# Batch 0 of a packed-attention kernel: its second softmax with tokens on the partitions, in two parts, and a new written order of the opening steps

## The chip, the core and the metric

The kernel runs on one core of a Trainium2 chip. The metric is the device time of one execution in microseconds (us). Shown times are medians of several runs. One more execution was recorded by the hardware profiler; its rows give the time inside the kernel, from the first instruction of the program (0 us).

The engines are named as in the profile: PE is TensorE (matmuls; PEld are its weight loads), DVE is VectorE, ACT is ScalarE, POOL is GpSimd, and SP is the engine whose queue issues the DMAs (SPq). Each takes its instructions in the order in which they were written.

## The reference

Eight batches, eight heads, 576 tokens, head dimension 64, and 32 packed queries `p` for each head:

```python
def sm_attn(qq, kk, vv):
    s = scale * np.matmul(qq, kk.transpose(0, 1, 3, 2))
    a = np.exp(s - np.max(s, axis=-1, keepdims=True))
    a = a / (np.sum(a, axis=-1, keepdims=True) + 1e-09)
    return np.matmul(a, vv)
p_packed = sm_attn(p, k, v)               # 32 x 64 for each head
out = sm_attn(q, p_packed, p_packed)      # 576 x 64 for each head
x = out.transpose(0, 2, 1, 3).reshape(8 * 576, 512)
result = (x @ w_a * (x @ w_b)) @ w_out    # w_a, w_b: 512 x 1536; w_out: 1536 x 512
```

All is fp32. The kernel multiplies in a faster matmul format (fp32r) and restores precision by splitting an operand into a high and a low part, so a product costs three matmuls: high by high, high by low, low by high.

## The kernel before, in words

**The algebra.** The second attention's output is never formed. Let `a2` be its softmax weights (256 rows, that is 8 heads by 32 packed queries, and 576 token columns, kept as two tiles `e` = 0, 1 of 128 rows). `p_packed` is multiplied into `w_a` and `w_b` once for each batch (G, `g_tiles`, high and low parts `ghi` and `glo`), and `a2` is multiplied by G (`mm1`). The 1536 hidden columns are cut into 12 tiles `ft` of 128. For each, `mm1` makes two products (one for w_a, one for w_b), ScalarE copies the first out of PSUM, VectorE multiplies it by the second, ScalarE rounds the high part `h_hi`, GpSimd makes the low part `h_lo`. `mm2` multiplies h by `w_out`.

**Batch 0** is written by its own list. Batches 0 and 1 use this plain form; later batches use another one and are not touched by the change.

**The steps.** `FIRST` is the order of the first loads on SP's queue: `p0`, `k0`, `k1`, `q0`, `q1` (four heads each, 512 KB), `k2`, `q2` (the last 64 tokens of all heads), `v0`, `v1`, and `w1` for one piece of the weights. `START` is the order in which the opening steps are written for all engines. In it:

- `k0`..`k4`, `q0`..`q4`: `turn_first`, TensorE turns a loaded piece and `TURN` says whether VectorE (0) or ScalarE (1) copies it out of PSUM. `T0`: p turned (`pT`). `P0`: p_packed turned (`ppT`).
- `S0`, `S1`, then `r0`, `r1` (four each): first softmax (`stage1`), for `e` = 0 and 1: scores; maximum and exponent; reciprocal of the sum; turns of the weights and two copies of them (`a1T`) on ScalarE; product with v, scaled into `pp`.
- `s0`, `s1` (seven each): the steps of the second softmax (`stage2`), one call for each `e`. Scores with the 32 packed queries of four heads on the partitions; a stream transpose by VectorE, so that the 32 values of a softmax lie side by side, and the maximum; subtraction; exponent on ScalarE; sum, reciprocal and the multiplication by it; a stream transpose back (`a2f`) and the high part of `a2` on ScalarE; the low part on VectorE (`lo_part`, L91). `SUBS` says whether subtraction and multiplication go to VectorE (1) or GpSimd (0).
- `A`, `B`, `C`: a weight piece comes as 64-bit numbers. `A` (high word) runs on ScalarE, `B` (low word) on the engine that `WAYS` gives for this piece (0 ScalarE, 1 VectorE, 2 GpSimd), `C` (`both_words`, L205) on VectorE. Each `C` frees a buffer and lets SP issue the next piece; twelve pieces fit. `D` splits a `w_out` piece.
- `W`: `warm`, dummy matmuls. `g`: G of the first two `ft` tiles, which needs the first four `C`. `Lk2`, `Lv2`, `Lp2` and the like: loads of batch 1.

After `START` the loop over `ft` begins. `mm1` calls `between()` twice for each `ft`; each call writes the steps that `PLAN_0` holds for that slot (weight pieces, batch 1's attention). At odd `ft`, `g_tiles` makes G for the next two tiles. For `ft` = 0, `mm1` first does the half of both products that needs `e` = 0 alone.

PSUM is held in three sets: `x` (two single banks), `m` (two pairs of banks), `s` (one pair). The order on every engine is the written one (a manual schedule); semaphores are added where data or a buffer must be waited for.

Of the kernel before, what the change touches and what calls it, by code (L numbers as in the profile page):

```python
# [12 lines left out]
ALU = mybir.AluOpType  # L13
# [6 lines left out]
def tile_packed_attn_gated_ffn(  # L20
# [69 lines left out]
    def lo_part(dst, src, hi, eng=nc.vector):  # L90
        return eng.tensor_tensor(out=dst, in0=src, in1=hi.bitcast(F32), op=ALU.subtract)  # L91
# [93 lines left out]
    def xT_cols(b, key, u, h, cols=slice(0, HS)):  # L185
        return xTs[b, key][h // R][64 * u:64 * u + 64, h % R, cols]
# [60 lines left out]
    def stage1(b, e):  # L247
# [59 lines left out]
            nc.vector.tensor_scalar(out=pp[b][:, i, :], in0=pps[:, 0:D], scalar1=rs, scalar2=None, op0=ALU.mult)  # L307
        yield

    def stage2(b, e):  # L310

        TU = 2 * XH
        x = bank_pair(b > 0 or e == 0)
        for r in range(R):
            for u in range(2):
                nc.tensor.matmul(  # L316
                    out=x[J * r:J * r + J, u, 0:HS], lhsT=ppT[64 * u:64 * u + 64, 1 if u ^ e else 2 * (b % 2), r, :],
                    rhs=xT_cols(b, "q", u, 2 * r + e), start=True, stop=True)
        yield
        s2 = work(b, f"s2_{e}", [P, TU, J], "t1")  # L320
# [6 lines left out]
        eng = nc.vector if b < 2 and SUBS[2 * b + e] == "1" else nc.gpsimd  # L327
        eng.tensor_tensor(out=s2, in0=s2, in1=mx.unsqueeze(2).broadcast_to([P, TU, J]), op=ALU.subtract)
# [5 lines left out]
        nc.vector.tensor_reduce(out=total, in_=s2, axis=AX, op=ALU.add)  # L334
        nc.vector.tensor_scalar(out=sum2, in0=total, scalar1=1e-9, scalar2=None, op0=ALU.add)
        nc.vector.reciprocal(out=sum2, in_=sum2)
        eng.tensor_tensor(out=s2, in0=s2, in1=sum2.unsqueeze(2).broadcast_to([P, TU, J]), op=ALU.mult)
# [12 lines left out]
        yield  # L350
# [27 lines left out]
                lo_part(lo, part, hi)  # L378


    def mm1_half(i, ft, ps=None, kts=range(E)):

        ps = bank_pair() if ps is None else ps
        cols = slice(P * i, P * i + P)
        steps = [(gt, at, kt) for kt in kts for gt, at in ((ghi, a2_hi), (ghi, a2_lo))]
        steps += [(glo, a2_hi, kt) for kt in kts]
        for n, (gt, at, kt) in enumerate(steps):
            for half in range(2):
                nc.tensor.matmul(  # L389
                    out=ps[:, half, 0:HS], lhsT=gt[:, kt, ft % 4, cols], rhs=at[:, kt, HS * half:HS * half + HS],  # L390
                    start=(n == 0 and kt == 0), stop=(n == len(steps) - 1 and kt == E - 1))
        return ps

    def mm1(b, ft, between):
        asb = sm.tile([P, 2, HS], F32, name="asb")
        if b == 0 and ft == 0:
            pa, pb = (mm1_half(i, ft, kts=(0,)) for i in range(2))
            mm1_half(0, ft, pa, (1,))
        else:
            pa, pb = mm1_half(0, ft), None  # L400
# [101 lines left out]
    WAYS = ("000000022220202120012012011200010010")  # L502
    TURN = ("0001110101")
    SUBS = ("0100")

    PLAN = (" |  |  | S0 | r0 | r0 |  | r0 |  | r0 Lv1 ; S1 | r1 | r1 q0 Lk2 | r1 | r1 | q1 Lk3 Lv2 P0 |  ; s0 | s0 s0 | s0 T2 | "
            "s0 Lp4 | s0 s1 | s1 s1 | s1 | s1 | s1 | t0 t1 t2 t3 u0 | k2 |  | k3 Lq2")
    PLAN = dict(enumerate(PLAN.split("|")))
    PLAN_0 = ("A | C C | B A B A | B C C B C | A A | C | B | C B A T0 k0 Lp2 A | A A B B C Lq0 | C C k1 | A B A | "
# [3 lines left out]
    PLAN_0 = dict(enumerate(PLAN_0.split("|")))  # L513

    pieces = [(c, n) for c in range(NC) for n in range(4)] + [(NC, f) for f in range(NFT)]
# [38 lines left out]
            del raws[c, n]  # L554
            load_pieces(2)

    def warm(n=9):

        x = bank_pair()[:, 0, :]
        t = firsts["k", 0].rearrange("p h t -> p (h t)")  # L560
        for _ in range(n):
            nc.tensor.matmul(out=x, lhsT=ident, rhs=t[:, 0:512], start=True, stop=True)
# [74 lines left out]
    for b in range(NB):  # L637
# [318 lines left out]
```

## Time and profile before

| | before |
|---|---|
| median of 3 runs | 714.15 us (713.82 to 714.51) |
| the profiled execution | 714.0 us |
| its span, first to last instruction | 712.2 us |
| PE, PEld busy | 699.0 us (98%), 574.2 us (81%) |
| DVE, ACT, POOL busy | 449.8 us (63%), 363.2 us (51%), 417.8 us (59%) |
| moved by DMA | 102.37 MB |

In the rows of the timeline the first number is the start in us, the second the time from the start of the first to the end of the last instruction that the row holds, then come engine, source line, operation, what is written from what, the shape and the count (x8 is eight instructions), and in brackets the idle time before it with what ended it. Busy times overlap on PE, since matmuls are pipelined. An fp32 matmul is two instructions, a turn by TensorE one. A row of the busy times by stretch has the stretch, its length, the busy time and count for PE, PEld, DVE, ACT and POOL, the granted clock, the share of the DMA engines and GB/s. A row of the chain of waits has start, duration, engine, tile and line. A row of the groups by line has the form, the count, the busy time and the mean duration in ns.

### The profile page before, as it was taken

Reading aid. Unit: us, or ns where it says so; the run is one execution under the profiler, and the core shown is the slowest. Engines: PE = TensorE matmul, PEld = TensorE weight load, DVE = VectorE, ACT = ScalarE, POOL = GpSimd, SP = SyncE. Lnnn points to the kernel's source line nnn. Section 1 sums busy time; section 2 is a strip of 40 time slices with the busy share of each in tenths; the row PEclk is TensorE's granted clock in tenths of the full one; section 3 lists DMA queues with packets and bytes.
Section 4 is the critical chain, followed back from the end, with each engine's and each line's share of the span. In section 5 each row is a group of like instructions: output and inputs, shape, how many; then the busy total and the mean of one; then the engine's idle time right before and its main releaser. Section 6 shows DMA issues by size and latency. Waiting matters only on the chain.

```text
span 712.2 us, 14198 instructions
## 1 busy us (share of the span) xinstructions
PE 699.0 (98%) x5558; PEld 574.2 (81%) x5558; DVE 449.8 (63%) x819; ACT 363.2 (51%) x733; POOL 417.8 (59%) x322
## 2 busy tenths in 40 slices
PE   6899999999999999999999999999999999999998
PEld 4488877888778887887888788788888888888887
DVE  3888755367455669665875668765785657754342
ACT  3788753554344455644563456554554455544520
POOL 0496753337334687745874579566776578856520
PEclk9999999999999999999999999999999999999999
DMA  8999872767344735555453574457146323133002
GB/s 230 387 274 315 220 162 53 193 153 282 93 98 139 211 96 141 139 138 146 134 111 115 142 195 93 106 176 182 61 98 180 105 89 119 61 110 127 1 1 74
DMA packets 177059, 102.37 MB, mean 144 GB/s; under 512 B 141280, under 2 KB 159456, under 8 KB 171616
## 3 DMA queue, kind: packets, MB, share of 16 engines
q1 hardware_dynamic: 176992, 101.47, 50.3%
q8 instruction: 43, 0.70, 0.4%
q14 instruction: 24, 0.20, 0.1%
HBM read 85.72 MB, written 15.73 MB: 142 GB/s over the span
## 4 chain that ended last, share of the span: by engine, by line
PE 94%; DVE 2%; SPq 1%; DMA 1%; ACT 1%; issue 0%; DVEq 0%; ACTq 0%
PE x L724 37%; PE m L765 29%; PE m L389 9%; PE x L779 5%; PE m L415 5%; PE s L301 2%; PE s L316 1%; PE s L255 1%; PE x L371 1%; PE s L291 1%; SPq L116 1%; DMA kn<-in_k_dram 1%; DMA nat<-in_k_dram 0%; PE m L152 0%; PE x L152 0%
## 5 line engine op out<-in xcount | busy, mean ns | idle before, releaser
L724 PE MATMUL x<-wo,h_hi 128*128 128x512 f32 (+1 forms) x776 | 249.3, 391 | 0.0
L91 POOL TENSOR_TENSOR h_lo<-asb,h_hi 128x576 fp32r<-128x576 f32 x96 | 140.3, 1462 | 83.3 <-ACT h_hi L810 44.6
L724 PEld LDWEIGHTS x<-wo,h_hi 128*128 128x128 f32 x776 | 140.8, 188 | 22.2 <-ACT gs L785 1.0
L724 PE MATMUL x<-wo,h_lo 128*128 128x512 f32 (+1 forms) x388 | 152.1, 392 | 0.0
L91 POOL TENSOR_TENSOR G_lo<-gs,G_hi 128x640 fp32r<-128x640 f32 x72 | 113.0, 1575 | 30.6 <-ACT G_hi L800 30.3
L724 PEld LDWEIGHTS x<-wo,h_lo 128*128 128x128 f32 x388 | 72.9, 188 | 11.8
L91 POOL TENSOR_TENSOR A_lo<-gs,A_hi 128x256 fp32r<-128x256 f32 x36 | 27.2, 754 | 89.7 <-ACT A_hi L788 89.7
L847 DVE TENSOR_TENSOR d<-m,d 128x576 f32<-128x576 f32 (+1 forms) x73 | 54.0, 740 | 34.6 <-ACT d L843 33.8
L860 DVE TENSOR_TENSOR asb<-m,d 128x288 f32<-128x288 f32 x72 | 32.4, 451 | 66.4 <-ACT c L856 64.8
L856 ACT COPY c<-m 128x288 f32<-128x288 f32 x72 | 28.8, 399 | 78.6 <-PE m L765 78.6
L734 DVE TENSOR_TENSOR part<-x,part 128x512 f32<-128x512 f32 (+1 forms) x65 | 44.1, 678 | 38.8 <-PE x L724 38.8
L765 PE MATMUL m<-tx_hi,G_hi 128*128 128x288 f32 x216 | 63.8, 296 | 0.0
L765 PE MATMUL m<-tx_hi,G_lo 128*128 128x288 f32 x216 | 63.7, 295 | 0.0
L785 ACT COPY gs<-x 128x512 f32<-128x512 f32 x36 | 21.1, 587 | 82.8 <-PE x L779 81.2
L765 PE MATMUL m<-tx_lo,G_hi 128*128 128x288 f32 x216 | 63.3, 293 | 0.0
L800 ACT CAST G_hi<-gs 128x640 fp32r<-128x640 f32 x72 | 52.2, 730 | 15.1 <-POOL gs L794 14.5
L843 ACT COPY d<-m 128x576 f32<-128x576 f32 (+1 forms) x73 | 46.6, 639 | 20.2 <-PE m L765 18.6
L810 ACT CAST h_hi<-asb 128x576 fp32r<-128x576 f32 x72 | 49.0, 680 | 11.5 <-DVE asb L874 11.5
L765 PEld LDWEIGHTS m<-a_hi,G_hi 128*128 128x128 f32 x144 | 27.0, 187 | 31.6 <-issue 17.4
L794 POOL TENSOR_TENSOR gs<-gs 128x512 f32<-128x512 f32 x36 | 46.7, 1296 | 2.6 <-DVE gs L791 2.5
L765 PE MATMUL m<-a_hi,G_hi 128*128 128x288 f32 x144 | 47.0, 326 | 0.0
L389 PE MATMUL m<-a_hi,ghi 128*128 128x288 f32 x192 | 43.2, 307 | 1.5 <-ACT ghi L377 1.5
(171 smaller groups left out, 1548.7 us busy)
## 6 DMA issues: line engine op xcount, KB each, us to landing
wr<-w_kept SPq DMA_DIRECT2D x36, 1024.0 KB
nat<-in_k_dram SPq DMA_DIRECT2D x56, 144.0 KB
nat<-in_q_dram SPq DMA_DIRECT2D x56, 144.0 KB
vt<-in_v_dram SPq DMA_DIRECT2D x28, 256.0 KB
out_dram<-part SPq DMA_DIRECT2D x27, 256.0 KB
raw<-in_moe_w_a_dram SPq DMA_DIRECT2D x12, 512.0 KB
raw<-in_moe_w_b_dram SPq DMA_DIRECT2D x12, 512.0 KB
raw<-in_moe_w_out_dram SPq DMA_DIRECT2D x12, 512.0 KB
```

Source lines behind the costliest of these rows:

```text
L91: return eng.tensor_tensor(out=dst, in0=src, in1=hi.bitcast(F32), op=ALU.subtract)
L389: nc.tensor.matmul(out=ps[:, half, 0:HS], lhsT=gt[:, kt, ft % 4, cols], rhs=at[:, kt, HS * half:HS * half + HS], start=(n == 0 and kt == 0 ...
L415: nc.tensor.matmul(out=o[:, cols], lhsT=ht[:, c0:c0 + P], rhs=wt[:, cols], start=(ft == 0 and n == 0), stop=(ft == NFT - 1 and n == 2))
L724: nc.tensor.matmul(out=o[:, cols], lhsT=ht[:, c0:c0 + P], rhs=wt[:, cols], start=(ft == fts[0] and n == 0), stop=end)
L734: nc.vector.tensor_tensor(out=parts[i][:, cols], in0=o[:, cols], in1=parts[i][:, cols], op=ALU.add)
L765: nc.tensor.matmul(out=bank[:, n % 2, 0:HS], lhsT=g, rhs=t, start=(first and i == 0), stop=(i == 2), skip_group_check=True)
L779: nc.tensor.matmul(out=gps[e][J * r:J * r + J, :], lhsT=ppT[rows, 2 * (b % 2), r, :], rhs=w[rows, r, :], start=True, stop=True)
L794: nc.gpsimd.tensor_tensor(out=gs[:, 2:4].rearrange("p a u f -> p a (u f)"), in0=gs[:, 0:2].rearrange("p a u f -> p a (u f)"), in1=s2.unsqu ...
L800: nc.scalar.copy(out=G_hi[:, n % 3], in_=gs[:, 1:6, n % 2])
L810: nc.scalar.copy(out=view(h_hi[ft]), in_=src)
L843: nc.scalar.copy(out=d[:, both], in_=X[:, both, 0:HS])
L847: nc.vector.tensor_tensor(out=d[:, both], in0=V[:, both, 0:HS], in1=d[:, both], op=ALU.add)
```

## The change

For batch 0 alone, `stage2` is replaced by `stage2_first`, called for part 0 and part 1 instead of `e` = 0 and 1. The tokens are now the stationary operand, so the scores come out of TensorE with 128 tokens on the partitions and 32 packed queries side by side; no stream transpose is needed. Part 0 has four of the nine groups of 64 tokens, part 1 the other five (`PARTS`). Maximum and subtraction are done by VectorE straight from PSUM, the multiplication by GpSimd (`SUBS` is all 0), and the result is turned by TensorE. The high and low parts of `a2` are taken from PSUM and now cover both `e` for a range of columns.

`mm1_part` does `ft` = 0 and 1 by these parts: first part 0 of both tiles, then G for tiles 2 and 3, then part 1 of both tiles. The other `ft` keep `mm1`, which loses its special case for `ft` = 0.

`FIRST`, `START`, `WAYS`, `TURN`, `SUBS` and `PLAN_0` are new strings. `START` holds 12 A, 13 B and 10 C in both kernels; `W` has 5 matmuls instead of 9.

```diff
+    PARTS = ((0, 4), (4, 9))
+    def stage2_first(part):
+        G = 4 + part
+        x = bank_pair(part == 0)[:, :, 0:2 * P]
...
+        for e in range(E):
+            for r in range(R):
+                for u in range(2):
+                    c = P * e + J * r
+                    nc.tensor.matmul(
+                        out=x[:, u, c:c + J], lhsT=qT(u, 2 * r + e, slice(P * part, P * part + P)), rhs=pT_of(u, e, r), ...)
+        if part:
+            y = bank()[:, 0:P]
...
+                        nc.tensor.matmul(
+                            out=y[o:o + TL, J * r:J * r + J], lhsT=qT(u, 2 * r + e, slice(2 * P, HS)), rhs=pT_of(u, e, r), ...)
+        yield
...     max (DVE) | yield | subtraction (DVE) | yield
+        nc.scalar.activation(out=s, in_=s, func=AF.Exp, scale=scale)
+        yield
+        nc.vector.tensor_reduce(out=sum2, in_=s, axis=AX, op=ALU.add)
...
+        eng.tensor_tensor(out=s, in0=s, in1=over(sum2), op=ALU.mult)
+        yield
...
+                nc.tensor.transpose(view[:, u], s2[:, 2 * u + e, :], ident)
+            if part:
+                nc.tensor.transpose(tps[e][:, 2 * P:2 * P + 64], s2[half, 4, :], ident[half, half])
...
+        nc.scalar.copy(out=hi, in_=a2)
+        yield
+        lo_part(lo, a2, hi)
+        yield
...
+    def mm1_part(ft, part):
+        x0, x1 = PARTS[part]
+        c0, n = 64 * x0, 64 * (x1 - x0)
+        ps = bank_pair()
...
+        steps = [(gt, at, kt) for gt, at in ((ghi, a2_hi), (ghi, a2_lo), (glo, a2_hi)) for kt in range(E)]
+        for i in range(2):
+            for k, (gt, at, kt) in enumerate(steps):
+                nc.tensor.matmul(
+                    out=ps[:, i, 0:n], lhsT=gt[:, kt, ft % 4, P * i:P * i + P], rhs=at[:, kt, c0:c0 + n], ...)
+        nc.scalar.copy(out=asb, in_=ps[:, 0, 0:n])
+        nc.vector.tensor_tensor(out=asb, in0=ps[:, 1, 0:n], in1=asb, op=ALU.mult)
+        nc.scalar.copy(out=hh, in_=asb)
+        lo_part(h_lo[ft][:, c0:c0 + n], asb, hh, nc.gpsimd)
...
-    FIRST = ("p0 k0 k2 k1 q0 v0 q1 v1 q2 w1 w1 w1 w1 w1 w1 w1 w1 w1 w1 w1")
-    START = ("T0 k0 k4 k1 k3 k2 q0 S0 S1 r0 r1 q1 r1 r0 r0 r1 r0 q2 r1 q3 q4 P0 s0 B s1 W A s0 B A A s0 s0 B s1 C "
-             "A s1 B s0 C s1 A s1 C B B Lp2 C A B A s0 s1 B C B B s0 B g A C A A s1 Lv2 Lk2 C C A A C B B Lk3 C s1")
-    WAYS = ("000000022220202120012012011200010010")
-    TURN = ("0001110101")
-    SUBS = ("0100")
+    FIRST = ("k2 k0 p0 k1 q0 w1 q1 v1 v0 w1 w1 w1 q2 w1 w1 w1 w1 w1 w1 w1")
+    START = ("k0 k4 T0 B k1 k3 k2 q0 S0 S1 r0 r1 q1 r0 q2 B r1 r1 B r0 q3 r0 r1 B A A A P0 s0 s0 q4 A B s1 W C s0 s0 "
+             "s1 C s0 s1 B A s1 C A C Lp2 s1 A s0 Lk2 B B A C s0 C A C C A g A B A s1 C B Lk3 B B C s1 B Lv2")
+    WAYS = ("222201010220012021210022011020000202")
+    TURN = ("1000101111")
+    SUBS = ("0000")
-    PLAN_0 = ("A | C C | B A B A | B C C B C | A A | C | B | C B A T0 k0 Lp2 A | ...")
+    PLAN_0 = ("A C C A C | | B B | A B C | A A B C | C Lp2 | B B | T0 A A | C A B k0 C A B | k1 | ...")
-    def warm(n=9):
+    def warm(n=5):
...
         for ft in range(NFT):
+            if b == 0 and ft < 2:
+                if ft == 1:
+                    g_tiles(b, (2, 3))
+                for f in range(2):
+                    mm1_part(f, ft)
+                    between()
+                continue
```

More of the change, by code (lines that the diff above doesn't have):

```diff
@@ L310, in stage2 @@
     def stage2(b, e):
         TU = 2 * XH
-        x = bank_pair(b > 0 or e == 0)
+        x = bank_pair(True)
         for r in range(R):
@@ L319, in stage2 @@
         yield
-        s2 = work(b, f"s2_{e}", [P, TU, J], "t1")
+        s2 = wk.tile([P, TU, J], F32, name="t1", bufs=2)
         nc.vector.transpose(out=s2.rearrange("p (u x) j -> p u (x j)", u=2), in_=x[:, :, 0:HS])
@@ L326, in stage2 @@
         yield
-        eng = nc.vector if b < 2 and SUBS[2 * b + e] == "1" else nc.gpsimd
+        eng = nc.vector if b == 1 and SUBS[2 * b + e] == "1" else nc.gpsimd
         eng.tensor_tensor(out=s2, in0=s2, in1=mx.unsqueeze(2).broadcast_to([P, TU, J]), op=ALU.subtract)
@@ L339, in stage2 @@
         halves = b >= NB
-        a2f = work(b, f"a2f_{e}", [P, 2, XH, TL], "t1" if halves and e else "t2")
+        a2f = wk.tile([P, 2, XH, TL], F32, name="t1", bufs=2) if halves and e else wk.tile([P, 2, XH, TL], F32, name="t2")
         nc.vector.transpose(out=a2f.rearrange("p u x l -> p (u x l)"), in_=s2.rearrange("p x j -> p (x j)"))
@@ L378, in g_tiles, with mm1_half @@
                 lo_part(lo, part, hi)
-    def mm1_half(i, ft, ps=None, kts=range(E)):
-        ps = bank_pair() if ps is None else ps
+    asb_of = {}
+    def mm1_part(ft, part):
+        assert part in first_of
+        x0, x1 = PARTS[part]
+        c0, n = 64 * x0, 64 * (x1 - x0)
+        ps = bank_pair()
+        if part == 0:
+            asb_of[ft] = sm.tile([P, 2, HS], F32, name="asb").rearrange("p u t -> p (u t)")
+        asb = asb_of[ft][:, c0:c0 + n]
+        steps = [(gt, at, kt) for gt, at in ((ghi, a2_hi), (ghi, a2_lo), (glo, a2_hi)) for kt in range(E)]
+        for i in range(2):
+            for k, (gt, at, kt) in enumerate(steps):
+                nc.tensor.matmul(
+                    out=ps[:, i, 0:n], lhsT=gt[:, kt, ft % 4, P * i:P * i + P], rhs=at[:, kt, c0:c0 + n],
+                    start=(k == 0), stop=(k == len(steps) - 1))
+        nc.scalar.copy(out=asb, in_=ps[:, 0, 0:n])
+        nc.vector.tensor_tensor(out=asb, in0=ps[:, 1, 0:n], in1=asb, op=ALU.mult)
+        hh = h_hi[ft][:, c0:c0 + n]
+        nc.scalar.copy(out=hh, in_=asb)
+        lo_part(h_lo[ft][:, c0:c0 + n], asb, hh, nc.gpsimd)
+    def mm1_half(i, ft):
+        ps = bank_pair()
         cols = slice(P * i, P * i + P)
-        steps = [(gt, at, kt) for kt in kts for gt, at in ((ghi, a2_hi), (ghi, a2_lo))]
-        steps += [(glo, a2_hi, kt) for kt in kts]
+        steps = [(gt, at, kt) for kt in range(E) for gt, at in ((ghi, a2_hi), (ghi, a2_lo))]
+        steps += [(glo, a2_hi, kt) for kt in range(E)]
         for n, (gt, at, kt) in enumerate(steps):
@@ L390, in mm1_half @@
                     out=ps[:, half, 0:HS], lhsT=gt[:, kt, ft % 4, cols], rhs=at[:, kt, HS * half:HS * half + HS],
-                    start=(n == 0 and kt == 0), stop=(n == len(steps) - 1 and kt == E - 1))
+                    start=(n == 0), stop=(n == len(steps) - 1))
         return ps
@@ L395, in mm1 @@
         asb = sm.tile([P, 2, HS], F32, name="asb")
[L396 to L400, printed above, removed]
+        pa = mm1_half(0, ft)
         nc.scalar.copy(out=asb, in_=pa[:, :, 0:HS])
         between()
-        pb = mm1_half(1, ft, pb, (1,) if pb is not None else range(E))
+        pb = mm1_half(1, ft)
         nc.vector.tensor_tensor(out=asb, in0=pb[:, :, 0:HS], in1=asb, op=ALU.mult)
@@ L475, in emit @@
                 if e == 0:
-                    st[b] = [stage1(b, 0), stage1(b, 1), stage2(b, 0), stage2(b, 1)]
+                    st[b] = [stage1(b, 0), stage1(b, 1)] + [stage2(b, i) if b else stage2_first(i) for i in range(2)]
                 next(st[b][e])
@@ L497, in tile_packed_attn_gated_ffn @@
     st = {}
[L499 to L507 removed]
+    FIRST = ("k2 k0 p0 k1 q0 w1 q1 v1 v0 w1 w1 w1 q2 w1 w1 w1 w1 w1 w1 w1")
+    START = ("k0 k4 T0 B k1 k3 k2 q0 S0 S1 r0 r1 q1 r0 q2 B r1 r1 B r0 q3 r0 r1 B A A A P0 s0 s0 q4 A B s1 W C s0 s0 s1 C s0 s1 B A s1 C A C Lp2 s1 A s0 Lk2 B B A C s0 C A C C A g A B A s1 C B Lk3 B B C s1 B Lv2")
+    WAYS = ("222201010220012021210022011020000202")
+    TURN = ("1000101111")
+    SUBS = ("0000")
+    PLAN = (" |  |  | S0 | r0 | r0 |  | r0 |  | r0 Lv1 ; S1 | r1 | r1 q0 Lk2 | r1 | r1 | q1 Lk3 Lv2 P0 |  ; s0 | s0 s0 | s0 T2 | s0 Lp4 | s0 s1 | s1 s1 | s1 | s1 | s1 | t0 t1 t2 t3 u0 | k2 |  | k3 Lq2")
     PLAN = dict(enumerate(PLAN.split("|")))
[L509 removed]
[3 rows of a table removed]
+    PLAN_0 = ("A C C A C | | B B | A B C | A A B C | C Lp2 | B B | T0 A A | C A B k0 C A B | k1 | B A | C C C | A C B Lq0 | S0 B C A | A B r0 | C C Lq1 | r0 D r0 A B A | B C B S1 D | B A C D | r1 C | r1 A D | A r0 T2 B | | C A B C D q0 r1 | B A C | Lv1 | r1 A D Lk3 | A B B D Lk2 q1 C P0 B C A A | C D Lp4 s0 | s1 s0 D B Lq2 s0 s1 D | | Lv2 s0 | s0 | s1 k2 s0 k3 | s1 | D | C s1 s0 Lq3 s1 s1")
     PLAN_0 = dict(enumerate(PLAN_0.split("|")))
```

43 lines of the change are left out of this document (added), and 3 rows, old and new, of the table PLAN_0.

## The prediction

> **What bounds the kernel now.** I read the page first, then the busy times by stretch, the chain of waits around the first big matmuls, and the queues row by row up to 45 us.
>
> ```profile
> span 712.2 us, 14198 instructions
> PE 699.0 (98%) x5558; PEld 574.2 (81%) x5558; DVE 449.8 (63%) x819; ACT 363.2 (51%) x733; POOL 417.8 (59%) x322
> ...
> 0.00:21.50 21.50, 13.92 (x190) 10.53 (x190) 7.23 (x18) 7.41 (x18) 0.70 (x6) 1.00 0.90 257
> 21.50:37.30 15.80, 13.72 (x81) 6.34 (x81) 14.70 (x25) 13.32 (x25) 10.00 (x6) 1.00 1.05 383
> 37.30:100.00 62.70, 62.47 (x557) 52.86 (x558) 48.24 (x74) 48.09 (x87) 43.94 (x27) 1.00 0.93 247
> 100.00:712.00 612.00, 608.92 (x4732) 504.47 (x4730) 379.63 (x703) 294.37 (x608) 363.22 (x284) 1.00 0.44 123
> ```
>
> From 37.3 us on TensorE works 62.47 of 62.70 us, then 608.92 of 612.00. So the end is set by when TensorE's unbroken run begins, and by stalls put into it. The change lies in the stretch before it. There VectorE is the full engine (14.70 of 15.80 us).
>
> ```profile
> 37.27 1.60 PE m L389 x10
> 38.87 1.11 PE x L371 x16
> ...
> 34.68 0.54 PE L389 MATMUL m<-a_hi,ghi 128*128 128x288 f32 x2 [1.48 <-ACT ghi L377]
> 37.27 0.54 PE L389 MATMUL m<-a_lo,ghi 128*128 128x288 f32 x2 [0.26 <-DVE a_lo L91]
> 43.22 0.52 PE L389 MATMUL m<-a_hi,ghi 128*128 128x288 f32 x2
> 34.66 1.29 DVE L91 TENSOR_TENSOR glo<-x,ghi 128x512 fp32r<-128x512 f32 x2
> ```
>
> The mm1 matmuls begin at 34.68 and stop once, until 37.27, for the last low part of `a2`, which VectorE writes late. Tile 2 begins at 43.22. That is my mark: what reaches TensorE by then is the same work in both kernels, so the mark moved is the end moved.
>
> **The change, step by step.** *Loads.* The first k load is issued second instead of fourth.
>
> ```profile
> 2.74 0.48 SPq L135 DMA_DIRECT2D kn<-in_k_dram  x1
> 3.26 0.50 SPq L139 DMA_DIRECT2D kn<-in_k_dram  x1
> 7.08 1.12 PE L152 MATMUL x<-ident,kn 128*128 128x128 f32 x4 [2.00 <-DMA kn<-in_k_dram]
> 10.03 1.92 PE L152 MATMUL m<-ident,kn 128*128 128x128 f32 x8
> 11.98 0.69 DVE L154 COPY xT<-m 128x512 f32<-128x512 f32 x1 [1.01 <-PE m L152]
> 20.50 0.44 PE L241 MATMUL x<-ident,pp 128*128 128x128 f32 x2
> 20.98 0.42 DVE L243 COPY ppT<-x 128x256 f32<-128x256 f32 x1 [0.29 <-PE x L241]
> ```
>
> SP starts at 0.74 in both. With only the 0.50 us issue ahead, k0 is issued near 1.26, 1.48 us sooner, and TensorE starts near 5.6. From there to 11.95 TensorE is the chain. T0 now stands inside it (0.45, as the two turns at 20.50), and k1 waits some 0.15 for a PSUM bank. The last k copy ends 0.88 earlier, at 11.8, and so do the first scores.
>
> ```profile
> 12.45 0.58 ACT L154 COPY xT<-x 128x512 f32<-128x512 f32 x1 [0.73 <-PE x L152]
> 16.20 0.58 ACT L293 COPY a1T<-x 128x512 f32<-128x512 f32 x1
> 16.68 0.26 ACT L294 COPY a1T<-x 64x128 f32<-64x128 f32 x1
> 17.05 0.90 PE L301 MATMUL x<-vt,a1T 128*32 128x64 f32 x40
> ```
>
> *ScalarE's order.* ScalarE is through with the exponents near 15.35, where the row at 16.20 came behind them before. But now the copies of q1 and q2 stand on ScalarE before the four copies of `a1T`. One such copy follows the other after 0.48, so two copies take 1.0. The `a1T` copies (1.45 for four) end at 17.85, the two groups of 40 matmuls (0.84 each) at 19.55, and with `pp`, the turn of 0.44 and the copy of 0.42 `ppT` is ready at 20.9 instead of 21.4. The lead is down to 0.5. v0 is now issued after w1 and v1. With it 4.0 MB are asked for; at the stretch's mean of 257 GB/s that is 15.7 us, and with 1 for the landing it is there before 17.85 and costs nothing; a later landing is paid in full.
>
> *Second scores.* Before: 16 matmul instructions, 288 columns through 32-column weights, 0.72. After: 32 instructions for part 0, 32 columns through 128-column weights, and as many for part 1, plus 32 with 32-column weights. The trace has no such form with 64 rows. The nearest has 32 rows:
>
> ```profile
> 19.30 0.66 PE L152 MATMUL m<-ident,qn 128*128 128x128 f32 x4
> 19.89 0.68 PE L157 MATMUL x<-ident,qn 32*128 32x32 f32 x8
> 21.55 0.72 PE L316 MATMUL s<-xT,ppT 64*32 64x288 f32 x16 [0.61 <-DVE ppT L243]
> ```
>
> Eight take 0.61 to the next row at 20.50, 76 ns each, all in one row group. Here two row halves alternate. If their loads run side by side, 32 take 1.2; one behind another, 2.4; the row at 21.55 (0.7) is the lower end. I take 1.2, because the groups of 40 at 17.05, on alternating column groups, need only 0.84/40 = 21 ns each. [...]
>
> *VectorE's list.* Durations go with elements: 512 cost 0.63 to the next instruction, 640 in two pieces 0.83.
>
> ```profile
> 25.33 0.71 DVE L205 SCALAR_TENSOR_TENSOR w_ab<-raw 128x512 uint32<-128x512 uint32 x1
> 25.93 0.78 DVE L328 TENSOR_TENSOR s<-s,mx 128x576 f32<-128x576 f32 x1
> 26.59 0.77 DVE L334 TENSOR_REDUCE sum<-s 128x18 f32<-128x576 f32 x1
> 27.40 0.18 DVE L335 TENSOR_SCALAR sum<-sum 128x18 f32<-128x18 f32 x1
> 29.81 1.08 DVE L337 TENSOR_TENSOR s<-s,sum 128x576 f32<-128x576 f32 x1
> 44.16 0.54 DVE L199 TENSOR_SCALAR raw<-raw 128x512 uint32<-128x512 uint32 x1
> ```
>
> VectorE loses four stream transposes (576 elements each, as at 25.93) and the multiplication at 29.81 (to GpSimd), and gains the subtraction of part 0 and, through WAYS, two B steps (0.5 each): about 2 us less. But eight C steps (0.63) now stand before `glo`, where five stood: 1.9 back. The list: scores of part 0 at 21.0 to 22.2, max 22.3; max, C, sub 1.9: 24.2. Part 1's scores are there (21.0 + 1.2 + 0.6 for q4 + 1.2 = 24.0, 24.1 seen). max 0.83, C 0.63: 25.66. exp of part 0 stands behind w5's low word on ScalarE: 6.3 MB, 5.5 of them by 21.5 and the rest at 383 GB/s, so by 23.4, less the 1.5 of the earlier start, plus 1 for the landing. So exp is done by 25.0. Then sum 1.05, sub 0.83, B 0.5, two C 1.26, sum 1.15, B 0.5, C 0.63, lo 0.63, three C 1.89, the two `glo` 1.29: 9.73, so 35.4 (before: 35.95).
>
> ```profile
> 23.46 7.99 PE L562 MATMUL m<-kn,ident 128*128 128x512 f32 x18
> 28.03 1.41 POOL L337 TENSOR_TENSOR s<-s,sum 128x576 f32<-128x576 f32 x1 [2.86 <-DVE sum L336]
> 35.00 2.94 ACT L194 ACTIVATE raw<-raw 128x512 f32<-128x512 f32 x5
> ...
> L724 PE MATMUL x<-wo,h_hi 128*128 128x256 f32 x16 | 2.9, 283 | 0.0
> L724 PE MATMUL x<-wo,h_lo 128*128 128x256 f32 x8 | 2.3, 283 | 0.0
> ```
>
> *Turns, GpSimd, ScalarE.* The multiplication by 1/sum, on GpSimd (1.41 for 576), of part 1 begins near 30.4 and ends at 32; its six turns take 0.9, to 33. ScalarE has five low-word steps in START instead of eight (0.57 each, 2.94 for five), and `ghi` is there near 33.5. All of it lies under VectorE's 35.4; without that cover `ghi` would be the start. W has five matmuls, ten instructions of 0.44 (7.99 for 18): it ends near 28.8, 0.8 after GpSimd's multiplication of part 0, and costs nothing as long as VectorE needs until 35.4; with all nine it would have ended at 32.3 and held up part 0's turns.
>
> *mm1 by parts.* 48 matmuls of 288 become 24 of 256 and 24 of 320. The 24 of 256 columns at the end take 2.9, 120 ns each; 288 cost 133 (ten in 1.33 of the 1.60 at 37.27); 320 by the same slope 147. 24 x (120 + 147) = 6.4 equals 48 x 133. Nothing gained or lost; the weight loads stay hidden at 256. TensorE does four matmuls on `ghi` (0.48) while `glo` is written, then from 35.45: 6.4 - 0.48, the g group 1.12, switches 0.3 (of the 5.95 from 37.27 to 43.22, 1.33 for ten, 1.12 and 3.2 for 24 are work): 42.8 against 43.22. Part 1's low half is two C and 0.83 behind `glo`, 37.6, and is wanted only at 39.5.
>
> *Batch 0 after that.* Moved steps, and three more B steps on GpSimd (12.54/5 = 2.5 each), cost nothing while TensorE is full and GpSimd has work for 43.94 of 62.70.
>
> ```profile
> 29.63 12.54 POOL L199 TENSOR_SCALAR raw<-raw 128x512 uint32<-128x512 uint32 x5 [0.19 <-DMA raw<-in_moe_w_b_dram]
> 35.77 1.67 SPq L215 DMA_DIRECT2D raw<-in_moe_w_a_dram  x2
> 40.88 6.74 SPq L116 DMA_DIRECT2D nat<-in_k_dram  x4
> ```
>
> Lk2, whose four issues held SP for 6.74 us, now goes ahead of w17 and w18, which were issued at 35.77. So these may come up to 6.7 later, while ScalarE takes w17 in slot 4, near 45. What waits behind it there is the copy of the next mm1 half; the second PSUM pair and a half tile of matmuls (1.6) cover it. I count 0; uncovered, 1 to 2 us (rival 4).
>
> **Sum.** -0.4 on the profiled execution's 714.0 us (1.8 outside its span), 0.15 below the median 714.15: 713.7 as a median. A measurement of this kernel tells 0.2% (1.43 us) from nothing, so: no change that can be told.
>
> **Rivals.**
> 1. *The weight loads queue up* (slower). At 76 ns one behind another, part 0 takes 2.4, and part 1 is there at 21.0 + 2.4 + 0.6 + 2.4 + 0.1 = 26.5 instead of 24.2 when VectorE wants it: +2.3, so 716.0. It decides from about 2.2 us a group on. For it: the L157 row, the only 128-column load with 32 columns. Against it: the L301 row. [...]
> 2. *TensorE's run starts warm earlier* (faster). The k turns take 0.23 us each at 10.03 (8 in 1.92), later 0.15 (four in 0.59, from 19.30 to 19.89). TensorE now starts at 5.6 without the 2.0 us hole before 7.08. If the fast rate comes near 9, VectorE's three k copies are the chain and end near 10.9, -0.9; the scores, alone 0.5 less at their lower end (0.7), come with it: 712.3. Against it: before, the turns were slow until 11.95, 4.9 us after 7.08; 4.9 after 5.6 is 10.5, past most turns.
> 3. *TensorE slows down again* (slower). With W ending near 28.8, TensorE is busy about 3 of the 7 us before its run. At half rate over the 4.9 us that it needed at the start it would lose 2.4: 716.1. Against it: no idle stretch over 2 us, and before it held over 1.48. [...]
> 4. *A load or ACT step comes late inside the run* (slower): w5, v0 or w17, 1 to 2 us: 715 to 716.
>
> **Chances.** Forecast, within 0.2%: 0.45. Rival 2, with any other gain over 1.43 us: 0.29. Rival 1: 0.13; rival 3: 0.05; rival 4: 0.08. The ends of the unknown costs, scores 0.7 (-0.5) and 2.4 (+2.3), an early clock (-0.9), loads (0.5 either way), give 711.9 to 716.1 as the range; the likeliest case alone 712.6 to 715.1.
>
> **What would show it.** First k turn near 5.6; `ppT` copied near 20.9; part 0's scores 1.2 us; VectorE without gaps from 24 to 35.4; first mm1 matmul near 33.5, `glo` ending near 35.4, tile 2 near 42.8; TensorE full after that. Wrong if `ppT` comes before 20 or after 21.5, if the scores take over 2 us, or if TensorE idles after 43.

## The result, and the profile after

The changed kernel takes 722.78 us (median of 4 runs, 721.07 to 724.43) against 713.99 us (713.82 to 714.51): a ratio of 1.0122, 95% interval 1.0095 to 1.0148. It is 8.8 us slower. Forecast were 713.7 us, with 711.9 to 716.1 as the range.

The page of the changed kernel, and then its busy times in two of the stretches that were shown of before (stretch, length, busy time and count of PE, PEld, DVE, ACT and POOL, granted clock):

```profile
span 720.2 us, 14346 instructions
PE 704.1 (98%) x5624; PEld 581.5 (81%) x5624; DVE 448.4 (62%) x818; ACT 361.6 (50%) x734; POOL 428.6 (60%) x328
```

```profile
21.50:37.30 15.80, 15.71 (x128) 10.35 (x126) 11.35 (x21) 6.73 (x14) 7.28 (x5) 0.68 1.03 372
37.30:100.00 62.70, 60.11 (x524) 51.01 (x528) 47.04 (x73) 49.78 (x95) 46.30 (x29) 0.97 0.83 230
```

VectorE, which was full from 21.5 to 37.3 us (14.70 of 15.80), now has work for 11.35. TensorE is busy for all of that stretch, at a mean clock of 0.68. The rows of the timeline of the changed kernel say why:

```profile
19.60 0.44 PE L241 MATMUL x<-ident,pp 128*128 128x128 f32 x2 [0.41 <-DVE pp L307]
20.55 2.56 PE L323 MATMUL s<-ppT,xT 64*128 64x32 f32 x32 [0.52 <-DVE ppT L243]
23.06 1.04 PE L157 MATMUL x<-ident,qn 32*128 32x32 f32 x8
24.03 3.62 PE L323 MATMUL m<-ppT,xT 64*128 64x32 f32 x32
28.16 6.45 PE L648 MATMUL m<-kn,ident 128*128 128x512 f32 x10
34.45 0.60 PE L370 MATMUL m<-ident,s 128*128 128x128 f32 x4
38.52 1.07 PE L467 MATMUL m<-a_hi,ghi 128*128 128x256 f32 x2 [1.31 <-ACT ghi L449]
43.36 1.09 PE L443 MATMUL x<-w_ab,ppT 64*32 64x512 f32 x16
48.51 0.53 PE L484 MATMUL m<-a_hi,ghi 128*128 128x288 f32 x2 [0.34 <-DVE asb L471]
23.15 0.69 DVE L345 TENSOR_REDUCE mx<-s 128x16 f32<-128x512 f32 x1 [2.65 <-PE s L323]
27.70 0.69 DVE L345 TENSOR_REDUCE mx<-m 128x16 f32<-128x512 f32 x1 [2.66 <-PE m L323]
38.51 1.28 DVE L91 TENSOR_TENSOR glo<-x,ghi 128x512 fp32r<-128x512 f32 x2
```

`ppT` comes 0.9 us earlier than before. Then part 1's scores take 3.62 us instead of the 1.2 of the forecast, VectorE waits 2.65 and 2.66 us for the scores, `glo` ends at 39.79, and tile 2 starts at 48.51 (before 43.22). So 5.3 us are lost by tile 2, and the span is 8.0 longer: 2.7 more go later.

The chain of waits of the changed kernel (start, duration, what; some rows left out at both ends) shows what lies between part 1's scores and the first mm1 matmul at 38.52, which waits 1.31 us for `ghi`:

```profile
24.10 3.56 PE m L323 x32
27.65 0.58 PE x L332 x32
28.23 6.38 PE m L648 x10
34.61 0.45 PE m L370 x4
35.08 0.59 ACT a_hi L376
35.67 0.60 ACT raw L202
36.27 1.72 ACT raw L194 x3
37.99 0.96 ACT ghi L449 x2
```

W (L648), begun at half clock (its instructions start 0.853 us apart from 29.18 to 31.74, and 0.429 apart from 32.30 on), holds part 0's turns to 34.45, and ScalarE's steps up to `ghi` follow. VectorE's `glo` ends at 39.79, and TensorE takes it at 39.81 without a wait. So two chains of nearly the same length lead into mm1, one over W and ScalarE, one over VectorE.

### The profile page after: what moved, and what is told of

It reads as the page before. It is cut to its first block, busy times and chain, and to the rows that moved or that the text cites. A ratio compares the mean times of both kernels' runs of the same rounds, so it can differ in the third digit from the quotient of the medians.

```text
span 720.2 us, 14346 instructions
## 1 busy us (share of the span) xinstructions
PE 704.1 (98%) x5624; PEld 581.5 (81%) x5624; DVE 448.4 (62%) x818; ACT 361.6 (50%) x734; POOL 428.6 (60%) x328
## 4 chain that ended last, share of the span: by engine, by line
PE 88%; DVE 3%; ACT 3%; DMA 2%; POOL 2%; issue 1%; SPq 1%; DVEq 0%; POOLq 0%; ACTq 0%
PE x L817 36%; PE m L858 29%; PE m L484 6%; PE x L872 5%; PE m L506 4%; PE s L301 1%; PE s L388 1%; PE s L255 1%; DMA wr<-w_kept 1%; PE m L648 1%; PE s L291 1%; DMA raw<-in_moe_w_out_dram 1%; POOL h_lo L91 1%; POOL raw L199 1%; POOL wo L91 1%
## 5 line engine op out<-in xcount | busy, mean ns | idle before, releaser
L91 POOL TENSOR_TENSOR h_lo<-asb,h_hi 128x576 fp32r<-128x576 f32 (+2 forms) x98 | 142.5, 1455 | 87.5 <-ACT h_hi L903 44.6
L966 DVE TENSOR_TENSOR m<-m,c 128x288 f32<-128x288 f32 x72 | 33.3, 463 | 17.7 <-PE m L858 16.0
```

The lines of the kernel that those rows point to most:

```text
L966: nc.vector.tensor_tensor(out=v, in0=v, in1=c2, op=ALU.add)
```

## The clock falls while TensorE is busy

Here the trace is cut every 3.41 us, counted from a change of its clock: in all 18 profiles of this case every change lies a whole number of 3.41 us from the others of its profile (10.24, 10.24, 6.83 and 3.41 us apart in the changed kernel). The busy times of the changed kernel by these spans:

```profile
18.35:21.76 3.41, 2.48 (x66) 1.99 (x64) 1.19 (x4) 1.44 (x3) 2.81 (x2) 1.00 1.07 318
21.76:25.17 3.41, 3.41 (x34) 3.28 (x32) 1.89 (x3) 1.03 (x4) 3.13 (x2) 0.50 1.06 367
25.17:28.59 3.42, 3.42 (x57) 3.29 (x57) 0.89 (x3) 1.58 (x3) 0.00 (x0) 0.50 1.05 383
28.59:32.00 3.41, 3.41 (x5) 1.34 (x5) 3.34 (x9) 0.94 (x2) 1.05 (x1) 0.50 1.05 387
32.00:35.41 3.41, 3.41 (x18) 1.50 (x25) 3.34 (x7) 1.28 (x3) 1.04 (x1) 1.00 1.03 374
35.41:38.83 3.42, 2.11 (x23) 0.86 (x7) 3.42 (x6) 3.42 (x8) 3.26 (x3) 1.00 0.86 258
38.83:42.24 3.41, 3.31 (x16) 3.23 (x16) 2.99 (x5) 3.41 (x7) 1.63 (x1) 0.50 0.76 125
```

And those of a run of the kernel before in which only W was changed, to small matmuls (further down):

```profile
22.64:26.05 3.41, 2.82 (x41) 1.73 (x42) 2.42 (x4) 3.01 (x6) 0.38 (x1) 1.00 1.05 386
26.05:29.46 3.41, 3.41 (x33) 3.41 (x32) 3.31 (x8) 2.60 (x5) 0.78 (x1) 1.00 1.05 386
29.46:32.88 3.42, 3.42 (x18) 3.42 (x17) 3.32 (x7) 3.42 (x7) 3.14 (x2) 0.50 1.05 386
```

The clock falls at 21.76 after a span in which PE was busy 2.48 of 3.41 us, and stays down through two spans of 3.41 of 3.41. Busy time does not decide here. What fits is the time in which columns stream through the array. It is an estimate: 0.87 ns for a column of an fp32 instruction (W before: 7.99 us for 18 of 512), 0.46 in mm1 (1.33 us for ten of 288), twice that at half clock (W's instructions: 0.853 and 0.429 us), and what overlaps counted once. By it the span before the fall at 21.76 streams 1.18 us, the two low ones 1.16 and 1.52, the one before the rise 3.29, and the one before the second fall 1.18. In the spans of the first 55 to 60 us of the 18 profiles, 20 of the 21 spans after which the clock fell stream 1.29 us or less (the other 1.53); the 184 after which it held stream 1.42 or more; it rose after 39 spans of 2.76 or more, and stayed low after 64 of 2.71 or less. Up to 700 us two profiles have one more fall, at 140.84 us in the first run below and at 186.38 in the run with fillers and q2's load; the spans before them stream 0.97 and 1.29 us. Two of the new scores' 32-column matmuls start 7 ns apart and stream 28 ns each by the estimate, and the next two start 112 ns after them at full clock: so the new scores stream for less than a third of the time that they take. In the changed kernel the clock rose at 32.00, while W (512 columns) ran; without W it stayed low to 44.50, into mm1.

## The experiments

Marks of the profiled executions in us: part 1's first maximum on VectorE, the end of `glo`, the start of the second and third g groups and of the first group on `wr`. Ratios are to the kernel before, with 95% intervals. The marks are of one execution, the medians of 4 to 10: the profiled one took 720.87 us with gap fillers and 725.35 with fillers and q2, 2.2 below and 4.1 above the median.

| kernel | part 1 | glo end | 2nd g | 3rd g | wr | median | ratio |
|---|---|---|---|---|---|---|---|
| before | | 35.95 | 38.80 | 46.60 | 177.31 | | 1 |
| after | 27.70 | 39.79 | 43.36 | 51.91 | 185.39 | 722.78 | 1.0122 (1.0095 to 1.0148) |
| gap fillers | 26.85 | 38.93 | 41.41 | 50.52 | 184.28 | 723.10 | 1.0115 (1.0091 to 1.0139) |
| old PLAN_0 | 28.61 | 40.68 | 43.17 | 52.09 | 183.22 | 720.17 | 1.0083 (1.0062 to 1.0105) |
| fillers, q2 | 25.52 | 37.60 | 42.01 | 50.41 | 185.98 | 721.28 | 1.0087 (1.0061 to 1.0112) |
| q2, old PLAN_0 | 27.68 | 39.79 | 42.27 | 51.18 | 182.32 | 719.99 | 1.0068 (1.0049 to 1.0087) |
| all three | 25.25 | 37.34 | 39.81 | 48.96 | 180.06 | 717.57 | 1.0040 (1.0024 to 1.0055) |
| four | 25.67 | 35.52 | 37.99 | 49.62 | 180.73 | 717.41 | 1.0037 (1.0025 to 1.0050) |

**Keeping the clock by idle matmuls.** `more()` is a matmul of 128 x 256 on TensorE whose result is not read; there are seven.

```diff
 turned(ppT, ...):  + more()
 stage2_first(0):   + more() ahead of and in the middle of the scores
 stage2_first(1):   + more() in the middle of the scores, and ahead of the last 32
 mm1_part(0, 0):    + more() twice
```

> The changed kernel with eight idle matmuls of 128 x 256 (128 x 128 weights, results never read) added on TensorE: one before the turn of pp, one before part 0's scores, one in the middle of each part's scores, one before the last 32 scores, two before the first mm1. Theory A (the granted clock falls because the new opening gives the array too little work, and the lost clock is the loss): the clock stays at 1.00 from about 11.5 us on, part 0's scores take 1.8 us plus the 0.43 of an idle matmul instead of 2.56, the five W matmuls 4.4 instead of 6.45, mm1 runs at full rate from its start, and tile 2 starts at 44 to 46 us instead of 48.5: 716 to 720 us, since the 2.7 us lost after tile 2 stay. Theory B (the new form itself is dear, the clock is a side effect): the idle matmuls only add their 2 to 3 us, tile 2 starts after 48, 723 to 726 us.

725.08 us, 1.0142 (1.0109 to 1.0174), with tile 2 at 51.00: the number that theory B gave. But the run does not decide between the two, since the fillers did not keep the clock. The clock held one span longer (to 24.79), since the span from 21.38 still streamed only 1.22 us, and then was low for 10.2 us; the matmuls inside the scores moved part 1's first maximum to 29.9. It narrowed theory A: a few more instructions don't keep the clock. Whether streamed time does is tried further down.

**The form alone, the order alone.** The first takes the new functions with every list of before; the second the old functions with the new lists.

```diff
 form:   FIRST, START, WAYS, TURN, SUBS, PLAN_0, warm(9) of before
 order:  before with the new FIRST, START, WAYS, TURN, SUBS, PLAN_0, warm(5);
         START: - "P0 s0 s0 q4 A B s1 W"  + "q4 P0 s0 s0 A B s1 W"
```

> The form alone: second softmax in two parts and the first two f tiles by parts, with the lists of loads and steps, the converting ways and the nine W matmuls of before. Theory A: the clock falls in the scores as in the changed kernel; nine W matmuls at half rate then last 8 to 12 us and hold part 0's turns to about 36: 720 to 726 us. Theory C (the new order of steps and loads is what costs): 713 to 715 us.

> The order alone: the old form of the second softmax and of tile 0, with the new lists of loads, steps and ways, five W matmuls, and q4's turn moved ahead of the scores, which need all columns here. Theory A: 16 matmuls of 288 columns keep the array at work, the clock stays at 1.00 until W is over; 712 to 717 us, with the 2.7 us lost after tile 2 in it if they come from the order. Theory C: 719 us or more.

Form alone: 722.52 us, 1.0114 (1.0099 to 1.0129). Its clock fell from 23.49 to 30.32, the nine W matmuls took 9.14 us, and part 0's turns came at 36.94, as theory A had it; the total is inside its range. Order alone: 727.48 us, 1.0180 (1.0165 to 1.0195), but the old form needs all of q, and its row names another cause:

```profile
23.75 1.03 PE L157 MATMUL x<-ident,qn 32*128 32x32 f32 x8 [4.65 <-DMA qn<-in_q_dram]
```

So it was run again with q2's load earlier (`SUBS` apart, the same edit):

```diff
-    FIRST = ("k2 k0 p0 k1 q0 w1 q1 v1 v0 w1 w1 w1 q2 w1 ...
+    FIRST = ("k2 k0 p0 k1 q0 w1 q1 v1 v0 q2 w1 w1 w1 w1 ...
     SUBS = "0100"
```

> The order alone once more, with q2's load ahead of the four w loads that stood before it, since the run of the order alone waited 4.65 us for q2, which the changed kernel wants later; the ways for the subtractions and the multiplications of part 1 as before (on VectorE). Theory A: TensorE streams enough up to the scores, clock at 1.00 there, 712 to 718 us, of which up to 3 are lost after tile 2. Theory C (the order costs by itself): 719 us or more, with the array starved by late loads.

721.83 us, 1.0105 (1.0087 to 1.0122): theory C's number. TensorE waited 1.67 us for ScalarE's copy of q4, GpSimd's and VectorE's new steps put the start of `glo` at 39.03 (34.66 before), and the clock fell twice. Each half of the change costs nearly as much alone as both together, and in each the clock falls. But their other losses differ: the nine W matmuls at half clock in the form alone, the wait for q4, the late `glo` and the new PLAN_0 in the order alone. So the halves don't add up, and these runs do not say what either costs within the whole change.

**The kernel before without W.**

```diff
-    START = ("... s1 W A s0 ...
+    START = ("... s1 A s0 ...
```

> The kernel before without its nine W matmuls (they compute nothing that is read). Theory A: between the scores at 23.5 and the g group at 31.6 TensorE has next to no work, the clock falls to half, and the g group and the first mm1 matmuls run at half rate for one or two spans of 3.4 us: 1.5 to 3.5 us more than before, 715.7 to 717.7. Rival (W is idle work that nothing depends on): 714, clock at 1.00.

The clock fell for 13.65 us, from 27.96 to 41.61, as theory A said, but the 1.5 to 3.5 us that it put on this did not come: the ratio is 1.0002 (0.9991 to 1.0013), so over ten executions it cost 0.9 us at most. In the profiled one (716.04 us, the median is 715.21) the third g group is 2.8 us late and the first group on `wr` 2.0. A lost clock can cost little, then; that it does so because TensorE is hardly waited for there (the low clock meets the g group and the first tile) is argued, not shown.

**Busy, but not streaming.** W of the kernel before, made of small matmuls:

```diff
-    def warm(n=9):   ... matmul(out=x, lhsT=ident, rhs=t[:, 0:512])
+    def warm(n=36):  ... matmul(out=x[:, 0:TL], lhsT=ident, rhs=t[:, 0:TL])
```

> The kernel before with W made of 36 matmuls of 32 columns (72 instructions, 128 x 128 weights each) instead of nine of 512; W computes nothing that is read. Theory A (streamed columns count, not busy time): TensorE is busy from 23.5 to 30 or so with weight loads, yet streams for about a quarter of the time; the clock falls to half near 25 to 30, and the run is 0.5 to 2 us slower, as without W. Rival (any busy TensorE keeps the clock): clock at 1.00, 714 us.

718.61 us, 1.0043 (1.0028 to 1.0058). Its rows by spans stand above: from 26.05 to 29.46 PE and PEld are both busy 3.41 of 3.41 us, the span streams 0.86 by the estimate, and the clock falls. So the clock fell here with only W changed, and after a span without idle time. The time is above the expected 2 us at most, since at half rate this W takes 11.55 us and holds the g group to 36.51 (31.63 before).

**Fillers only where TensorE waits.**

```diff
 turned(ppT, ...):  + more()
 stage2_first(0):   + more() ahead of the scores
```

> The changed kernel with two idle matmuls of 128 x 256 (results never read) only where TensorE waits anyway: one before the turn of pp, one before part 0's scores. Theory A, as the runs so far narrow it: what lowers the clock is a span of 3.41 us in which columns stream through the array for less than about 1.2 to 1.4 us; a wait counts, but so do weight loads. Then the span that ends near 21.8 holds over 1.8 us and the clock falls one span later, near 25; the scores of part 1 are there at 25 to 25.5 instead of 27.7, and tile 2 starts 1 to 3 us earlier than in the changed kernel: 719 to 722 us. Theory B (the form, not the clock): the fillers change nothing or add 0.4: 722.5 to 724.

723.10 us, theory B's number: as slow as the changed kernel in the median. The profiled execution (720.87 us) kept its clock to 27.04 (mean 0.998) and was 1.1 us shorter; the other three had 0.990 to 0.993. Its rows show the next thing behind the clock:

```profile
21.37 1.97 PE L330 MATMUL s<-ppT,xT 64*128 64x32 f32 x32
24.25 0.65 PE L157 MATMUL x<-ident,qn 32*128 32x32 f32 x8 [0.91 <-DMA qn<-in_q_dram]
24.83 1.98 PE L330 MATMUL m<-ppT,xT 64*128 64x32 f32 x32
```

At full clock a group of 32 takes 1.97 us, and q4's turn now waits 0.91 for the late load of q2.

**Without W**, and **with the old list for batch 0's slots**:

```diff
-    START = ("... s1 W C s0 ...        -    PLAN_0 = ("A C C A C | | B B | ...
+    START = ("... s1 C s0 ...          +    PLAN_0 = ("A | C C | B A B A | ...
```

> The changed kernel without its five W matmuls. Theory A: part 0's turns start when GpSimd is through, 31 to 32 us, instead of 34.45, but TensorE streams little until mm1, the clock stays at half until some 3.4 us into mm1, and mm1 begins little earlier, since VectorE's list still ends near 38: tile 2 at 47 to 50, 721 to 725 us. Rival (W at half rate is what holds the start up): tile 2 at 45 to 46, 719 to 720 us.

> The changed kernel with the list of steps for batch 0's slots (PLAN_0) as it was before. Theory: the kernels with the new list lose 2.1 to 4.7 us between the third g group and the first group on wr, those with the old one lose nothing there. So the old list gives 719.0 to 720.8 us with tile 2 still near 48.5. Rival (the loss after tile 2 only follows from the late start, since due times are missed): 722 to 724 us.

Without W: 722.33 us, 1.0101 (1.0079 to 1.0124). Part 0's turns started at 32.72 instead of 34.45, but the clock stayed low to 44.50, VectorE's `glo` ended at 40.96, and nothing was won (tile 2 at 49.68). From part 1's maximum VectorE took 12.09 us to the end of `glo`, as with W, and that is now the chain that bounds. So the run shows that W alone does not hold the start up; what W cost and what it gave back by raising the clock it does not tell apart. Old PLAN_0: 720.17 us, as expected, by the ratios 2.8 less than the changed kernel, and the third g group is no earlier. In the profiles the stretch from the third g group to the first group on `wr` is 132.8 to 135.6 us in the seven kernels with the new list and 129.9 to 131.1 in the eleven with the old. The new list's largest single loss is on the chain of waits of the changed kernel (start, duration, what):

```profile
172.02 6.61 PE m L484 x48
178.63 0.02 issue
178.65 6.61 DMA wr<-w_kept
185.26 0.14 issue
185.39 1.10 PE x L872 x16
```

Before, this transfer was issued at 171.96 and TensorE, with other work in front, reached it at 177.31 without a wait; after, TensorE waits 1.3 us for it and 0.7 for the copy behind it. With the old list neither wait is there. Which of the moved steps makes the transfer late was not tried.

**The missing combinations, and all three together** (fillers, q2's load one w load earlier, old PLAN_0):

> The changed kernel with the two idle matmuls in TensorE's waits and q2's load one w load earlier; the new list of steps stays. Theory D (clock 2 to 2.5 us, q2 0.5 to 0.9, new list 2.2 to 2.6): part 1's first maximum on VectorE at 25.2 instead of 27.7, 719 to 720.5 us. If the list of steps alone carries the loss: 722 to 723.

> The changed kernel with q2's load one w load earlier and the old list of steps, without the idle matmuls. Theory D: the clock falls near 21 to 24 as in the changed kernel, part 1's first maximum at 27 to 28, 719 to 720.5 us. If the clock costs nothing by itself: 717.5, as with all three.

> The changed kernel with three of the suspected losses taken away together: the two idle matmuls in TensorE's waits (as in the run with fillers), the old list of steps for batch 0's slots, and q2's load one w load earlier, so that q4's turn does not wait for it. Theory D (the loss is a sum: a lost clock of 2 to 3 us, 2 to 2.5 us by the new list of steps, 0.9 us by q2's late load, the rest by the new form's own length on TensorE and VectorE): 716 to 719 us, tile 2's g group near 40.5 to 43. Theory A (the clock alone): 714 to 715 when the clock stays. Rival (they overlap and bring nothing together): 720 us or more.

721.28 (0.8 us above what theory D gave), 719.99 and 717.57 us. By the ratios (0.1% is 0.71 us) the three together give back 5.9 us of 8.7, inside theory D's range; 2.9 us remain. Put in last, the old list is worth 3.4 us and the fillers 2.0. q2's load on top of the fillers comes to 2.0 and the fillers without it to 0.5; neither of these two can be told from nothing by the intervals, and q2's load was not put in last. Clock and time go together inside one kernel too: the six runs with fillers and q2 took 719.13 and 720.37 us at a mean granted clock of 0.998, 721.26 to 721.41 at 0.993 to 0.995, and 725.35 at 0.988. Which of the two drives the other this does not say: the last of them is at half clock for 6.83 us more from 186.38 on, right after TensorE waited 1.97 us for `wr`.

**Four C and three A steps moved behind the g group**, on top of the three:

```diff
-    "... s0 Lk2 B B A C s0 C A C C A g A B A s1 C B ..."
+    "... s0 Lk2 B B s0 g A C A C C A C A B A s1 C B ..."
```

> As the run with three losses taken away, and the four C steps and three A steps that stand between part 0's turns and the g group moved behind it, so that VectorE writes glo some 1.9 us sooner and ScalarE writes ghi 1.8 us sooner. Theory D: 1 to 2 us less than with three, 715 to 717 us. If VectorE's list did not bound the start of mm1: the same as with three.

717.41 us, no change, where theory D wanted 1 to 2 us less. The second g group starts at 37.99, even ahead of before, but VectorE does the same C steps a little later, and TensorE waits there:

```profile
35.43 4.30 DVE L205 SCALAR_TENSOR_TENSOR w_ab<-raw 128x512 uint32<-128x512 uint32 x6
40.86 0.56 PE L474 MATMUL m<-a_hi,ghi 128*128 128x320 f32 x2 [1.36 <-DVE asb L478]
```

So moving the C steps moved the wait. But VectorE alone does not bound this stretch: from 20 us to the third g group it has 24.94 us of work and 1.66 idle in the kernel before, 22.57 and 9.34 in the changed one, 22.68 and 6.94 here. The chain of waits runs by turns over VectorE's C steps and ScalarE's copies out of PSUM, behind which VectorE waits 1.29 and 1.63 us. With all three losses away it runs first over W (25.66 to 31.72, again begun at half clock) and then over ScalarE. What the last 2.9 us are was not taken apart; no run leaves W out there.

**Part 1's multiplication on VectorE**, on top of the three:

```diff
-    SUBS = ("0000")
+    SUBS = ("0100")
```

> As the run with three losses taken away, and part 1's multiplication by 1/sum on VectorE (640 elements, near 1.1 us) instead of GpSimd (1.26). Theory E (VectorE stands still for the whole of GpSimd's multiplication: the C step issued beside it took 1.76 instead of 0.68): VectorE's list does not get longer, the C step falls back to 0.68, and the time is that of the run with three, 717 to 718. Rival (the two run side by side, the long C step has another cause): VectorE's list gets 1.1 longer, 718.5 to 719.

719.30 us, 1.0052 (1.0033 to 1.0071): just above the rival's number, but the interval overlaps the one with three, and in the profiled executions the clock fell earlier (at 23.47, not 25.37), so the time decides nothing. The rows say more. The changed kernel:

```profile
34.37 1.26 POOL L361 TENSOR_TENSOR s<-s,sum 128x640 f32<-128x640 f32 x1 [2.88 <-DVE sum L359]
34.42 1.76 DVE L205 SCALAR_TENSOR_TENSOR w_ab<-raw 128x512 uint32<-128x512 uint32 x1
```

This run:

```profile
34.31 0.83 DVE L368 TENSOR_TENSOR s<-s,sum 128x640 f32<-128x640 f32 x1
35.48 0.68 DVE L205 SCALAR_TENSOR_TENSOR w_ab<-raw 128x512 uint32<-128x512 uint32 x1
```

A C step issued while GpSimd multiplies takes 1.76 us instead of 0.68: it ends 0.55 us after GpSimd's multiplication, as in all eight profiles in which the two meet like this (1.759 to 1.765 us). So theory E is right about the cause of the long step. That VectorE stands still for the whole of GpSimd's instruction agrees with the rows of this multiplication, 1.08 us here. It does not agree with those of GpSimd's low-word step (L199, one input): of 193 C steps that began while one ran, in the first 200 us of the 18 profiles, the longest took 1.27 us, and 126 ended before it did.

Theory E's other half did not come. VectorE's list from part 1's maximum to the end of `glo` did not stay at 12.09 us, it is 12.49: the multiplication itself takes 0.83, and two C steps now meet a low-word step that GpSimd, with less to do, begins earlier. The changed kernel, then this run:

```profile
31.69 1.28 DVE L205 SCALAR_TENSOR_TENSOR w_ab<-raw 128x512 uint32<-128x512 uint32 x2
```

```profile
31.26 1.73 DVE L205 SCALAR_TENSOR_TENSOR w_ab<-raw 128x512 uint32<-128x512 uint32 x2
```

**The new form with the old lists and fillers**, and **the first k load ahead of p in the kernel before**:

```diff
 form alone, more() as in the run with fillers, warm(5)
-    FIRST = ("p0 k0 k2 ...      +    FIRST = ("k0 p0 k2 ...
```

> The new form alone (old lists of loads, steps and ways, as in the run of the form alone) with the two idle matmuls in TensorE's waits and five W matmuls instead of nine. Theory A and D: the clock holds one span longer, W no longer holds part 0's turns to 36.9, tile 2 some 3 to 5 us earlier than in the form alone: 716 to 720 us. If the form's own instructions cost the 8 us: 721 us or more.

> The kernel before with one swap in the list of loads: the first k load ahead of p's three. TensorE's first k turn moves from 7.08 to near 6, T0 waits for p instead. If the start of the chain counts in full: 712.5 to 713.5 us; if T0, whose load comes later and which stands first on TensorE, holds the k turns back: 714 us, no change.

717.63 us, 1.0046 (1.0030 to 1.0062): by the ratios 4.9 less than the form alone, so there too the clock and the long W, taken away together, were most of the loss. The swap of loads: 714.32 us, 0.9994 (0.9983 to 1.0006): no change that can be told; the second g group is 0.7 earlier in its profile. No run points to a version that beats the kernel before.

## Why the prediction was wrong, step by step

It put tile 2 at 42.8; it came at 48.51. The 5.7 us split along its own steps, and 2.7 us come behind them.

1. *Loads and ScalarE's order: right.* The first k turn was at 5.12 (forecast 5.6), `ppT` copied by 20.49 (20.9). v0 came in time; the 1 us for its landing was an estimate, which this does not measure. q2, which the forecast did not look at, became the late load where the scores were faster (0.91 us with fillers).
2. *Second scores: the step that failed.* Forecast 1.2 us a group and part 1 at 24.2; it came at 27.70, 3.5 late. 1.05 of it is the form at full clock (25.25 with all three losses away): a group takes 1.97, as against 0.72 for a group of the form before. The alternating row halves do overlap (the two loads of a pair start 7 ns apart), but a pair needs 0.112 us at full clock, nearer to the L157 row than to the L301 row that I chose. The other 2.45 us are the half clock: the four profiles whose clock held through part 1's scores, without a wait for q2, have part 1 at 25.25 to 25.78, the six in which it fell, without fillers inside the scores, at 27.27 to 28.88.
3. *VectorE's list: 0.9 short.* Forecast 11.2 us from part 1's maximum to the end of `glo`, measured 12.09 in the changed kernel and with all three: GpSimd's multiplication, counted as hidden work, holds a C step of VectorE for 1.08. Done by VectorE itself it would have been no cheaper (12.49).
4. *mm1 by parts: right at full clock.* At full clock 12 pairs of 320 columns take 0.29 us each, as forecast (2 x 147 ns), and tile 2 follows the end of `glo` after 7.36 us with all three (forecast 7.4). After the change it was 8.72: the second fall, 38.83 to 42.24, costs 1.3.
5. *W and what follows it: W without cost was right as far as the run without it shows, the cover was wrong.* W ended near 34.6 instead of 28.8. So `ghi`, forecast near 33.5 and meant to lie under VectorE's list, let the first mm1 matmul start only at 38.52; VectorE's list ended so late that this added little.
6. *Batch 0 after that, counted at 0: wrong by about 2.7*, shown by the old PLAN_0.

So the outcome was rival 3, *TensorE slows down again*, which I gave 0.05 and 716.1, with a dear form and a dear list on top. Its own mechanism, too little work ahead of mm1, is only the second fall (1.3 us); the first came while TensorE was busy with the scores. I dismissed it by "no idle stretch over 2 us", as if only idle time lowered the clock; the trace of before, at 1.00 from 11.88 to 711.61 us, did not show that. The measurement differs: the run with W of small matmuls shows a fall at 29.46 after a span without any idle time (PE and PEld busy 3.41 of 3.41 us). Rival 1, the weight loads, was half right: 2 us a group, near the 2.2 where it was to decide. Rival 4, a late load inside the run, came in kind, though with another load, `wr`, and far behind the loads that it names. Rival 2 did not come: the clock rose at 11.52 instead of 11.88, worth nothing behind the other steps.

## What to carry to other kernels

Before making matmuls narrow, add up by spans of a few us (3.41 here) how long columns will stream, not how long TensorE will look busy: here the clock fell after a span with PEld busy 3.41 of 3.41 us and 0.86 streamed by the estimate. And look at which engine waits for the next matmul: 13.65 us at half clock cost 0.9 us at most in one kernel here. An engine that looks free is no free place for work if its instruction stops a full one: count that stop (1.08 us here) against what the work would cost there (0.83). When losses overlap, undo them together and one by one: alone, the fillers here looked worthless, and the form and the order each looked like the whole loss.

## What the runs showed of the hardware that I had not expected

- With W of small matmuls the clock fell after a span of 3.41 us with PE and PEld busy throughout (streamed 0.86 by the estimate). In the first 55 to 60 us of the 18 profiles it held after every span above 1.53 and rose only after 2.76 or more. From 1.42 to 1.53 both outcomes occur, so these runs tell no better where the clock falls.
- Loads for the two row halves overlap (7 ns from the first start to the second), yet 32 alternating 64 x 128 loads with 32 columns take 1.97 us at full clock, 3.62 at half: a pair each 112 and 213 ns. Eight 32 x 128 loads with 32 columns in one row group (the L157 rows) start 62 to 63 ns apart at full clock, once they run, and 107 at half.
- A VectorE step with two operands took 1.76 us instead of 0.68 when GpSimd's multiplication was under way; beside GpSimd's low-word step it took 1.27 at most (193 steps).
